# Linear attention feeding an MLP: steps 9 to 12 of the attention in three visits to TensorE instead of four

## The chip, the cores and the metric

The kernel runs on one NeuronCore of a Trainium2 chip. The metric is the time of one execution on the device in microseconds (us), as the median of several runs; lower is better.

## What is computed

The inputs are q, k and v of shape (4, 8, 768, 64) (batch, heads, positions, head size), a decay `lam` per head, and two weight matrices of 512 x 2048 and 2048 x 512. Block by block of 64 positions a causal linear attention with decay is taken, which carries a state of 64 x 64 per batch and head:

```python
for b in range(nb):
    sl = slice(b * block, (b + 1) * block)
    qb, kb, vb = (q[:, :, sl], k[:, :, sl], v[:, :, sl])
    intra = np.einsum('bhic,bhjc->bhij', qb, kb) * Dmask[None]
    intra = np.einsum('bhij,bhjd->bhid', intra, vb)
    inter = np.einsum('bhid,bhde->bhie', qb * lam_pow[None], kv_state)
    out[:, :, sl] = intra + inter
    kb_dec = kb * rev_pow[None]
    kv_state = lam_block * kv_state + np.einsum('bhsd,bhse->bhde', kb_dec, vb)
```

Its output, as 3072 rows of 512, goes through `gelu_tanh(x @ w_in) @ w_out`, and that is the result.

## The kernel before

**The attention** is cut into 24 steps. Step s holds 256 positions of one batch for four of the eight heads; an even step and the odd one after it are the two halves of the heads. Three pairs of steps make a batch (`NSB` = 3), so steps 6 to 11 are batch 1, and steps 10 and 11 are its last positions. Inside a step, two chunks c = 0 and 1 of 128 positions follow each other through the state.

A step is made of: loads of q, k and v (`load_step`, all issued by SP's DMA queue); a scaling of q into fp16 on DVE and a copy of k on ACT (`cast_q` L282, `cast_k` L295); a scaling of v on POOL (`scale_v` L266); a transpose of q and k by DMA into a `qkT` tile (L303); the scores on TensorE (`scores` L350, two PSUM banks); the causal mask (`causal` L360, two DVE instructions, one for each bank); the outputs, that is masked scores times v (L399, or L436 in a burst), and the old state times q (L408, or L461); k times v for the new state (L385, or L450); the state update (`update`: `t` on DVE L506 and `u`, its masked fp16 copy, on POOL L513); and a copy of the outputs to an `xT` tile on ACT (`x_out` L487). For the last positions of a batch the second chunk's k times v is not computed.

TensorE visits the attention in one of two ways. `R(n, s)` (L902) is a single visit: scores of step n, k times v of step n, outputs of an earlier step s, with two banks for the scores and two (`OK`) for the rest. `burst(ns, ss)` (L415) takes several steps together: the scores of all steps in `ns`, then the outputs of all steps in `ss`, then k times v of all in `ns`, then the old states; its tiles are two banks of scores per step, two `O` and two `K`. Within a visit most matmuls use 64 x 64 tiles of the array, four of them at a time; the old states (L408, L461) and the whole MLP use 128 x 128.

**The MLP** works on groups of steps: group 0 is steps 0 to 3, group 1 steps 4 and 5, group 2 steps 6 and 7, group 3 steps 8 to 11, and so on. A group is queued as soon as its outputs are there (`queue_group` L544), as a list of pieces (`filler`). Groups 1 and 2 have eight pieces of the first matrix (`mm1` L557: 8 matmuls of 128x256 into one `Hps` bank, then a gelu on ACT, L565) and seven pieces of the second (`product` L616, a Winograd scheme: 8 matmuls of 128x256 each, L640). The products come in the order 1, 2, 5, 6, 3, 7, 4. Products 1, 6, 7 and 4 add up in one and the same bank, `MX`: after 1, 6 and 7, and at the end after 4, ACT copies the sum out (L657), and each of these products waits for the copy before it. Products 2 and 5, 3 use the banks `MW` and `MY`. `sum_g` (L610) makes sums of gelu results on DVE for the products, `sum_win` (L151) sums of the first matrix on DVE for the last two groups.

**The order** is written by hand: the kernel body is a sequence of calls, and `fill(n)` (L898) puts the next n pieces of the queue at its place. Every engine works through its own instructions in that order. All PSUM tiles come from one pool of eight banks, `ps_M`; a new tile waits for the readers of the tile that had its bank.

The change lies in the loop of L1017 to L1058, which handles steps 8 to 12:

```python
FILL = {8: (2, 0, 0, 0), 9: (1, 2, 1, 2), 10: (0, 1, 1, 3), 11: (0, 1, 1, 3), 12: (0, 2, 1, 3)}
for n, (a, b, c, d) in FILL.items():
```

For n = 9 this puts product 6 of group 1 ahead of the preparation of step 11, then products 3 and 7, then the visit `R(9, 8)`, then product 4 and two `Hps` pieces of group 2. One more `Hps` piece leads to `R(10, 9)`, five more to `R(11, 10)`, products 1, 2, 5, 6, 3 and 7 of group 2 to `R(12, 11)`, and product 4 follows that one.

Of the kernel before, what the change touches and what calls it, by code (L numbers as in the profile page):

```python
# [15 lines left out]
def kernel(  # L16
# [10 lines left out]
    nc = tc.nc  # L27
# [108 lines left out]
    def w_in_block(t, cs, fs):  # L136

        if t in I_SUMS:
            return wi_sum[(t - 1) // 2][:, (t - 1) % 2, cs, fs]
        F, C = t  # L140
        return w_in16[:, 2 * C + cs.start : 2 * C + cs.stop,
                      F * DFF // 2 + fs.start : F * DFF // 2 + fs.stop]

    def sum_win(m, j, eng):

        if not wi_sum:
            wi_sum.extend(wst.tile([P, 2, 2, DFF // 2], FP16, tag=f"w{2 + i}", name=f"ws{i}")
                          for i in range(2))
        a, op, b = I_SUMS[m]
        cs, fs = slice(0, 2), slice(512 * j, 512 * j + 512)  # L150
        pin(eng.tensor_tensor(w_in_block(m, cs, fs), w_in_block(a, cs, fs),  # L151
                              w_in_block(b, cs, fs), op))
# [116 lines left out]
    def prep_qk(s):  # L269
        cast_qk(s)  # L270
        transpose_dma(s)
# [5 lines left out]
    def cast_q(s):  # L277
        q32 = ld32[s][0]
        tqk = a16p.tile([P, 2, 2, HH, D], FP16, tag="qk16", name=f"qk16_{s}")
        tq, tk = tqk[:, 0], tqk[:, 1]  # L280
        q_eng = nc.gpsimd if s == 3 else nc.vector
        pin(q_eng.tensor_tensor(wide(tq), q32[:], decay(dq, s), ALU.mult))  # L282
        if s == 0:
            inverse(halves[0])
            odd(halves[1])
            inverse(halves[1])
        a16[s] = (tq, tk)
        whole_qk[s] = tqk
# [50 lines left out]
    def half64(i):  # L339
        return slice(64 * i, 64 * i + 64)  # L340
# [3 lines left out]
    def scores(n):  # L344
        o = qkT[n]
        Sps = [ps_M.tile([P, 2, 2, P], FP32, tag="M", name=f"S{hl}") for hl in range(2)]
        for hp in range(2):
            for jk in range(2):
                for hl, c in TILES:
                    pin(nc.tensor.matmul(  # L350
                        Sps[hl][half64(c), hp, jk, :], o[half64(hl), 1, jk, hp, half64(c)],
                        o[half64(hl), 0, :, hp, half64(c)], start=True, stop=True,
                        skip_group_check=True))
        Ss[n] = Sps

    def causal(n):

        t = ptp.tile([P, 2, 2, 2, P], FP16, tag="PT", name=f"PT_{n}")
        for hl, Sps in enumerate(Ss.pop(n)):
            pin(nc.vector.tensor_tensor(  # L360
                t[:, hl].rearrange("p b c d -> p b (c d)"), Sps[:].rearrange("p b c d -> p b (c d)"),
                mask[:].unsqueeze(1).to_broadcast([P, 2, 2 * P]), ALU.mult))
        PTs[n] = t
# [51 lines left out]
    def burst(ns, ss, *mix, ahead=None):  # L415


        for i, n in enumerate(ns):
            scores(n)
            if ahead and i == 0:  # L420
                ahead()
        O = [ps_M.tile([P, 2, 2, P], FP32, tag="M", name=f"O{c}") for c in range(2)]
        seen = set()

        def start(kind, c, hl):
            new = (kind, c, hl) not in seen
            seen.add((kind, c, hl))
            return new

        qTs = [qkT.pop(s) for s in ss]  # L430
        for i, s in enumerate(ss):
            PT, tv = PTs.pop(s), a16.pop(s)[2]
            for hp in range(2):
                for jk in range(2):
                    for c, hl in TILES:
                        pin(nc.tensor.matmul(  # L436
                            O[c][half64(hl), i, hp, :], tv[half64(c), jk, 2 * hp + hl, :],
                            PT[half64(c), hl, hp, jk, :], start=start("O", c, hl), stop=False,
                            skip_group_check=True))
        if ns:  # L440
            K = [ps_M.tile([P, 2, P], FP32, tag="M", name=f"K{c}") for c in range(2)]
        for i, n in enumerate(ns):
            _, tk, tv = a16[n]
            last = (n // 2) % NSB == NSB - 1
            for jk in range(2):
                for hp in range(2):
                    for c, hl in TILES:
                        if c == 1 and last:
                            continue
                        pin(nc.tensor.matmul(  # L450
                            K[c][half64(hl), i, hp * D : hp * D + D],
                            tk[half64(c), jk, 2 * hp + hl, :], tv[half64(c), jk, 2 * hp + hl, :],
                            start=start("K", c, hl), stop=(jk == 1), skip_group_check=True))
            Kps[n] = [t[:, i] for t in K]
        for i, s in enumerate(ss):
            for c in range(2):
                if c == 0 and (s // 2) % NSB == 0:
                    continue
                u = us.pop((s, 0) if c else (s - 2, 1))
                for hp in range(2):  # L460
                    pin(nc.tensor.matmul(O[c][:, i, hp, :], u[:, hp].rearrange("p l d -> p (l d)"),  # L461
                                         qTs[i][:, 0, :, hp, half64(c)], start=False, stop=True,
                                         skip_group_check=True))
        for n in ns:
            causal(n)
        for i, s in enumerate(ss):
            x_out(s, [t[:, i].rearrange("p h t -> p (h t)") for t in O])
        sbg = ss[-1] // 2
        g, i = group_of[sbg]
        if ss[-1] % 2 == 1 and i == len(groups[g]) - 1:  # L470
            queue_group(g, *mix)
        for n in ns:
            update(n, 0)

    def x_out(s, OK, second=None):
        sbg, half = divmod(s, 2)
        g, i = group_of[sbg]
        if g not in xT:
            xT[g] = xtp.tile([P, 2, len(groups[g]), 2, SB], FP16, tag="xT", name=f"xT_{g}")
        dst = xT[g][:, half, i]  # L480
        for c in range(2):
            d = dst[:, :, c * P : (c + 1) * P].rearrange("p hp (t j) -> p hp j t", j=2)
            o = OK[c][:, 0:256].rearrange("p (hp j t) -> p hp j t", hp=2, j=2)
            if c == 1 and second is not None:
                pin(second.tensor_copy(out=d, in_=o))
            else:
                pin(nc.scalar.activation(out=d, in_=o, func=AF.Copy))  # L487
# [410 lines left out]
    def fill(n):  # L898
        for _ in range(min(n, len(filler))):
            filler.pop(0)()  # L900

    def R(n, s, ahead=None, keep=False):  # L902

        if n is not None:
            scores(n)
        if ahead:
            ahead()
        products(n, s)
        if n is not None:
            causal(n)  # L910
        if s is not None and s % 2 == 1:
            g, i = group_of[s // 2]
            if i == len(groups[g]) - 1 and g > 0:
                queue_group(g)
        if n is not None and not keep:
            update(n, 0)

    def U(n):
        update(n, 1)
# [98 lines left out]
    for n, (a, b, c, d) in FILL.items():  # L1018
        stage_t(n)
        fill(a + (n == 10))  # L1020
        if n == 8:
            cast_q(n + 2)
            fill(1)
            cast_k(n + 2)
            transpose_dma(n + 2)
        else:
            prep_qk(n + 2)
        if n < 11:
            load_step(n + 4, "qkv" if n < 10 else "qk")
        if n == 9:  # L1030
            store_pair(1)
        if n == 11:
            scale_v(13)
            load_step(14, "v")
            load_step(16, "qk")
        elif n == 9:
            scale_v(11)
        elif n == 10:
            scale_v(12)
            load_step(15, "qk")  # L1040
        elif n == 12:
            scale_v(14)
        fill(b + (n == 8) - (n == 10))
        R(n, n - 1, keep=n == 8)
        fill(c)
        if n == 8:
            update(n, 0)
            scale_v(n + 2)
            fill(2)
        U(n)  # L1050
        if n == 12:
            prep_qk(15)
            load_step(15, "v")
            load_step(16, "v")
            scale_v(15)
        fill(d)
        if n > 8:
            sum_win((n - 7) // 2, (n - 1) % 2, nc.vector)  # L1058

    cast_qk(16)  # L1060
    load_step(17, "qk")
# [91 lines left out]
```

## Time and profile before

| | |
|---|---|
| median of 5 runs | 198.88 us (198.76 to 199.51) |
| the profiled execution | 199.11 us |
| its span | 197.3 us, 5913 instructions |
| TensorE busy | 191.5 us, 97% of the span, granted clock 1.00 |
| VectorE (DVE) busy | 153.4 us, 78% |
| ScalarE (ACT) busy | 121.9 us, 62% |
| GpSimd (POOL) busy | 73.4 us, 37% |
| single visits R(9, 8), R(10, 9), R(11, 10), R(12, 11) begin at | 63.99, 68.51, 73.90, 80.16 us |
| stage from 59 to 69 us, busy of 10 us | PE 10.0, DVE 9.46, ACT 5.40, POOL 6.87 |

Times in the profile are of one execution, from the span's start. PE is TensorE, PEld its weight loads, SPq the DMA-issuing queue of SyncE. A timeline row gives start, duration, engine, line, operation, output and inputs, and the number of instructions merged into it; a bracket behind it is the idle time of the engine and what ended it. Matmuls overlap, so the time that a block of them takes is read from the starts of neighbouring rows.

### The profile page before, as it was taken

What the parts mean: (1) busy time and instruction counts of PE and PEld (TensorE: products, weight loads), DVE (VectorE), ACT (ScalarE), POOL (GpSimd) and SP (SyncE); (2) the same over time, 40 slices, a digit from 0 to 9 for tenths busy, and PEclk for the clock granted to TensorE, in tenths of its full rate; (3) what the DMA queues carried; (4) which work ended last, traced back from release to release, by engine and by line L of the source; (5) the groups of instructions that cost most, each with busy time, mean ns of one, the idle gap of its engine ahead of it and who ended that gap; (6) DMA issues with size and microseconds to landing.
All of it is one profiled execution on the core that took longest, in us unless ns stands there. A gap on an engine that the chain in (4) does not pass through costs nothing.

```text
span 197.3 us, 5913 instructions
## 1 busy us (share of the span) xinstructions
PE 191.5 (97%) x2429; PEld 139.9 (71%) x2431; DVE 153.4 (78%) x297; ACT 121.9 (62%) x249; POOL 73.4 (37%) x85
## 2 busy tenths in 40 slices
PE   8979999999999999999999999999999999999993
PEld 2546544456888888654688764578888888888882
DVE  4798632789999889849999947998778996588620
ACT  3664877457774685676845378844768845779221
POOL 6594213557554931069754507165002030002000
PEclk9999999999999999999999999999999999999999
DMA  5999999999999999999996998400220300030205
GB/s 170 293 325 385 385 386 385 286 285 293 253 222 243 261 342 224 214 242 278 234 293 139 270 310 203 93 6 0 53 81 28 107 7 0 0 110 0 106 19 197
DMA packets 62810, 38.13 MB, mean 193 GB/s; under 512 B 18624, under 2 KB 55744, under 8 KB 62784
## 3 DMA queue, kind: packets, MB, share of 16 engines
q1 hardware_dynamic: 62240, 37.50, 74.0%
q8 instruction: 19, 0.31, 0.7%
q10 hardware_dynamic: 544, 0.26, 0.5%
q14 instruction: 7, 0.06, 0.1%
HBM read 27.26 MB, written 6.29 MB: 170 GB/s over the span
## 4 chain that ended last, share of the span: by engine, by line
PE 78%; DMA 12%; SPq 6%; DVE 1%; issue 1%; ACT 0%
PE Hps L561 21%; PE MX L640 18%; PE MY L640 9%; PE HX L739 7%; DMA wi<-in_moe_w_in_dram 7%; DMA k<-in_k_dram 5%; PE MW L640 4%; SPq L70 4%; PE HY L739 4%; PE S L350 3%; PE O2ps L576 3%; PE HW L739 2%; SPq L94 2%; PE OK L408 1%; PE O L461 1%; PE O L436 1%
## 5 line engine op out<-in xcount | busy, mean ns | idle before, releaser
L561 PE MATMUL Hps<-xT,w_in 128*128 128x512 f16 (+1 forms) x288 | 50.5, 332 | 0.0
L513 POOL TENSOR_TENSOR u<-t,lumask 128x256 f16<-128x256 f32 x40 | 30.9, 787 | 41.8 <-DVE t L506 24.1
L561 PEld LDWEIGHTS <-w_in 128*128 128x128 f16 x288 | 27.9, 98 | 19.1 <-DVE w_in L110 0.2
L565 ACT ACTIVATE gT<-Hps 128x512 f16<-128x512 f32 x56 | 33.5, 598 | 11.6 <-PE Hps L561 11.1
L360 DVE TENSOR_TENSOR PT<-S,mask 128x512 f16<-128x512 f32 x48 | 30.3, 681 | 6.7 <-PE S L350 6.7
L266 POOL TENSOR_TENSOR v<-v,dv 128x512 f16<-128x512 f32 x24 | 28.2, 1179 | 15.8 <-DMA v<-in_v_dram 15.5
L640 PEld LDWEIGHTS <-gs 128*128 128x128 f16 x320 | 31.2, 98 | 3.6
L640 PEld LDWEIGHTS <-gT 128*128 128x128 f16 x240 | 23.3, 98 | 3.2 <-ACT gT L565 0.2
L640 PE MATMUL MX<-w_sum,gs 128*128 128x256 f16 x160 | 21.4, 273 | 0.0
L282 DVE TENSOR_TENSOR qk<-q,dq 128x512 f16<-128x512 f32 x23 | 19.9, 867 | 1.3 <-DMA q<-in_q_dram 1.3
L692 POOL TENSOR_TENSOR o<-u,q 128x512 f32<-128x512 f32 (+1 forms) x5 | 5.8, 1154 | 35.1 <-ACT u L657 35.1
L295 ACT ACTIVATE qk<-k 128x512 f16<-128x512 f32 x23 | 14.4, 625 | 7.2 <-DMA k<-in_k_dram 7.0
L610 DVE TENSOR_TENSOR gs<-gT 128x1024 f16<-128x1024 f16 (+1 forms) x24 | 16.2, 681 | 1.5 <-ACT gT L565 1.5
L576 PE MATMUL O2ps<-w_out,gT 128*128 128x512 f16 x64 | 14.6, 379 | 0.0
L487 ACT ACTIVATE xT<-OK 128x256 f16<-128x256 f32 x26 | 9.9, 452 | 6.7 <-PE OK L408 6.2
L739 PEld LDWEIGHTS <-ws 128*128 128x128 f16 x128 | 12.5, 97 | 1.8
L657 ACT ACTIVATE u<-MX 128x256 f32<-128x256 f32 x18 | 6.9, 383 | 10.2 <-PE MX L640 10.2
L487 ACT ACTIVATE xT<-O 128x256 f16<-128x256 f32 x22 | 8.0, 461 | 5.4 <-PE O L461 4.5
L350 PEld LDWEIGHTS <-qkT 64*64 64x64 f16 x384 | 6.0, 106 | 6.9 <-issue 3.2
L576 PEld LDWEIGHTS <-gT 128*128 128x128 f16 x64 | 6.1, 98 | 6.6
L640 PE MATMUL MY<-w_out,gs 128*128 128x256 f16 x80 | 10.7, 273 | 0.0
L640 PE MATMUL MX<-w_sum,gT 128*128 128x256 f16 x80 | 10.4, 273 | 0.0
(96 smaller groups left out, 317.7 us busy)
## 6 DMA issues: line engine op xcount, KB each, us to landing
q<-in_q_dram SPq DMA_DIRECT2D x24, 256.0 KB, 5.1
k<-in_k_dram SPq DMA_DIRECT2D x24, 256.0 KB, 5.2
v<-in_v_dram SPq DMA_DIRECT2D x23, 256.0 KB, 5.2
out_dram<-o SPq DMA_DIRECT2D x23, 256.0 KB, 4.0
wo<-in_moe_w_out_dram SPq DMA_DIRECT2D x4, 1024.0 KB, 9.4
wi<-in_moe_w_in_dram SPq DMA_DIRECT2D x4, 512.0 KB, 7.1
wi<-in_moe_w_in_dram SPq DMA_DIRECT2D x2, 1024.0 KB, 12.9
v<-in_v_dram ACTq DMA_DIRECT2D x1, 256.0 KB, 4.1
```

The costliest lines, as they stand in the source:

```text
L266: pin(nc.gpsimd.tensor_tensor(wide(tv[:]), ld32[s][2][:], decay(dv, s), ALU.mult))
L282: pin(q_eng.tensor_tensor(wide(tq), q32[:], decay(dq, s), ALU.mult))
L295: pin(nc.scalar.activation(out=wide(tk), in_=k32[:], func=AF.Copy))
L360: pin(nc.vector.tensor_tensor(t[:, hl].rearrange("p b c d -> p b (c d)"), Sps[:].rearrange("p b c d -> p b (c d)"), mask[:].unsqueeze(1).t ...
L487: pin(nc.scalar.activation(out=d, in_=o, func=AF.Copy))
L513: pin(nc.gpsimd.tensor_tensor(u[:], state[half][:].unsqueeze(2).to_broadcast([P, 2, 2, D]), lumask[:, 2 * half : 2 * half + 2, :].unsqueez ...
L561: pin(nc.tensor.matmul(by_block(Hps[:, i, :]), w_in16[:, c, f * P : (f + 1) * P], x(c), start=(c == 0), stop=(c == NC - 1)))
L565: pin(nc.scalar.activation(out=dst, in_=Hps[:], func=AF.Gelu_apprx_tanh))
L576: pin(nc.tensor.matmul(O2[tau][0][:], gT[:, f % HF, f // HF, tau * P : (tau + 1) * P], w_out16[:, f, :], start=(n == 0), stop=(n == NF - 1)))
L610: pin(nc.vector.tensor_tensor(g_rows(m, i), g_rows(a, i), g_rows(b, i), op))
L640: pin(nc.tensor.matmul(dst, lhsT, rhs, start=(opens and i == 0), stop=(closes and i == HF - 1), skip_group_check=True))
L739: pin(nc.tensor.matmul(dst[:, i, :], w_in_block(a, slice(c, c + 1), slice(f * P, f * P + P))[:, 0], x_block(b, slice(c, c + 1))[:, 0], sta ...
```

## The change

Visit 9 is dropped. At n = 9 only the pieces, the preparation of step 11 and the sums stay. At n = 10 a burst takes the scores of 9 and 10 and the outputs of 8, and both second-chunk updates come after the next piece. At n = 11 a burst takes the scores of 11 and the outputs of 9 and 10. The visit of n = 12 stays. One `sum_win` moves from n = 10 to n = 9.

```diff
         fill(b + (n == 8) - (n == 10))
-        R(n, n - 1, keep=n == 8)
+        if n == 10:
+            burst((9, 10), (8,))
+        elif n == 11:
+            burst((11,), (9, 10))
+        elif n != 9:
+            R(n, n - 1, keep=n == 8)
         fill(c)
         if n == 8:
             update(n, 0)
             scale_v(n + 2)
             fill(2)
-        U(n)
+        if n == 10:
+            U(9)
+        if n != 9:
+            U(n)
...
         fill(d)
-        if n > 8:
-            sum_win((n - 7) // 2, (n - 1) % 2, nc.vector)
+        if n == 9:
+            sum_win(1, 0, nc.vector)
+            sum_win(1, 1, nc.vector)
+        elif n > 10:
+            sum_win(2, n - 11, nc.vector)
```

## The prediction, made before the result was known

> **What bounds the kernel now.** I read the page first (busy time, chain), then the waits of PE, then PE's timeline in the stage of the change, then ACT, DVE and POOL there. Page:
>
> ```profile
> PE 191.5 (97%) x2429; PEld 139.9 (71%) x2431; DVE 153.4 (78%) x297; ACT 121.9 (62%) x249; POOL 73.4 (37%) x85
> ...
> PE 78%; DMA 12%; SPq 6%; DVE 1%; issue 1%; ACT 0%
> ```
>
> PE is busy 97% of the span and is most of the chain. All the waits of PE:
>
> ```profile
> PE S L350 <- DVE qkT L326: 0.9, 1, 0.9
> PE idle L181 <- PEq L1137: 0.8, 1, 0.8
> PE Tps L321 <- POOL qk L282: 0.4, 1, 0.4
> ```
>
> All three lie before 14 us. Behind that there is no gap in which a later delay could vanish, or from which something could be won: what PE gains or loses at 60 to 80 us stays in the span. PE's timeline around the visit of step 9 (start, us, instruction):
>
> ```profile
> 62.15 1.04 PE L640 MATMUL MY<-w_out,gs 128*128 128x256 f16 x8
> 63.02 1.04 PE L640 MATMUL MX<-w_sum,gs 128*128 128x256 f16 x8
> 63.99 0.42 PE L350 MATMUL S<-qkT 64*64 64x128 f16 x16
> 64.24 0.29 PE L385 MATMUL OK<-v,qk 64*64 64x64 f16 x16
> 64.36 0.40 PE L399 MATMUL OK<-PT,v 64*64 64x128 f16 x16
> 64.69 0.40 PE L408 MATMUL OK<-qkT,u 128*128 128x128 f16 x4
> 64.92 1.04 PE L640 MATMUL MX<-w_sum,gT 128*128 128x256 f16 x8
> ```
>
> The starts tell the time, since the ends overlap. Eight product matmuls take 63.02 - 62.15 = 0.87. The visit takes 64.92 - 63.99 = 0.93, and its first score starts 63.99 - 63.02 - 0.87 = 0.10 later than another product would. The MX rows on both sides are products 7 and 4 of group 1, in one bank. Between them ACT copies that bank:
>
> ```profile
> 64.10 0.39 ACT L657 ACTIVATE u<-MX 128x256 f32<-128x256 f32 x1 [0.84 <-PE MX L640]
> ```
>
> The visit covers this copy: it ends at 64.49, and product 4 begins at 64.92.
>
> **What the Trainium skill says.** "TensorEngine Tiling (Array Packing)", Key Properties: changing the tiling mode drains TensorE. The trace agrees: 0.10 on the way from 128*128 into 64*64, and some 0.11 on the way out (below). "PSUM — Partial Sum Buffer", PSUM bank collisions: two engines must not be in one bank and quadrant at once, so software orders them by semaphores. So product 4 must wait for the copy; in the trace of before that wait is never the last, so none of its rows shows a price. "Perfetto Trace Analysis", Per-engine timelines: ACT's row ends with the write acknowledged, the semaphore's way to another engine comes after it, and a matmul's row starts behind its wait. The only row that shows that way is a DVE one, 0.06:
>
> ```profile
> 12.01 0.41 DVE L326 COPY qkT<-Tps 128x512 f16<-128x512 f16 x1
> ```
>
> ```profile
> 12.48 0.42 PE L350 MATMUL S<-qkT 64*64 64x128 f16 x16 [0.91 <-DVE qkT L326]
> ```
>
> 12.01 + 0.41 = 12.42, and the score starts at 12.48. "TensorE: Matmul & The Clock Gate", HAM oscillation: only idle gaps above some 3.4 us slow PE's clock. Here the granted clock is 1.00 through the 0.91 gap too, so I give a gap of under 1 us no further cost.
>
> **The change part by part.** The matmuls are the same; they stand in two visits in place of three (step 12's is untouched).
>
> 1. *What a visit costs beside its matmuls.* The timeline of a burst of before with two steps in and two out:
>
> ```profile
> 116.49 0.64 PE L350 MATMUL S<-qkT 64*64 64x128 f16 x32
> 116.97 0.62 PE L436 MATMUL O<-PT,v 64*64 64x128 f16 x32
> 117.41 0.42 PE L450 MATMUL K<-v,qk 64*64 64x64 f16 x32
> 117.77 0.62 PE L461 MATMUL O<-qkT,u 128*128 128x128 f16 x8
> 118.22 7.07 PE L561 MATMUL Hps<-xT,w_in 128*128 128x512 f16 x32
> ```
>
> Sixteen scores cost 0.48 / 2 = 0.24 (0.25 in a single visit), 16 outputs 0.22, a state matmul (L461) 0.45 / 8 = 0.057. Sixteen K matmuls cost 64.36 - 64.24 = 0.12 where outputs follow; 32 of them here, before L461, take 0.36, which is 2 x 0.12 and 0.11 for the way back to 128*128. The same 0.11 is in the single visit: 0.33 for 16 outputs. Eight K matmuls of a last block use half the tiles and cost as much as 16: visits of steps 10 and 11, with 8, take 0.93 too.
> Burst of 9 and 10 with outputs of 8: S 0.47, O 0.22, K 0.25, way out 0.11, four states 0.23: 1.28. Burst of 11 with outputs of 9 and 10: 0.25 + 0.44 + 0.12 + 0.11 + 0.46 = 1.38. With two ways in: 2.66 + 0.20 = 2.86. Before: 3 x 0.93 + 0.30 = 3.09. Saved: 0.23.
>
> 2. *The bank wait inside a burst.* A burst takes eight tiles of a pool of eight banks, so its K1 needs the bank of the last Hps piece ahead of it, whose gelu runs 0.11 to 0.71 behind the burst's start. K starts at 0.47 + 0.22 = 0.69; with 0.06 for the signal it is 0.08 late. The burst of 13 and 14 has the same pattern: its gelu and its K rows are
>
> ```profile
> 87.35 0.60 ACT L565 ACTIVATE gT<-Hps 128x512 f16<-128x512 f32 x1 [0.27 <-PE Hps L561]
> ```
>
> ```profile
> 87.94 0.50 PE L450 MATMUL K<-v,qk 64*64 64x64 f16 x32
> 88.37 0.28 PE L461 MATMUL O<-qkT,u 128*128 128x128 f16 x2
> ```
>
> 0.43 for K in place of 0.36. I take 0.07 for the burst of 9 and 10 (bounds 0 and 0.15); the burst of 11 has long finished pieces ahead of its banks. Saved is now 0.23 - 0.07 = 0.16 (bounds 0.05 and 0.30).
>
> 3. *The cover that goes.* The visit of step 9 is where the single visit stood between products 7 and 4. With it gone, product 4 follows product 7 at once: it would start at 63.02 + 0.87 = 63.89. But the copy still cannot begin before product 7's last matmul is through, 64.10, and ends at 64.49; with 0.06, product 4 starts at 64.55. PE stands still for 0.66. Bounds: 0.60 (a signal that takes nothing) and 0.75 (0.15 for it). Queued behind it on PE are three Hps pieces and the burst; ACT's gelus, DVE's causal rows and so everything of the later stages wait for those. The same pair of group 2 keeps its cover, the untouched visit of 12 (79.20 product 7, 80.16 visit, 81.10 product 4).
>
> 4. *What is moved on the other queues, taken at nothing.* DVE: causal 9 (2 x 0.64) and its four state updates go behind two ws sums (L151, one moved forward from step 10) and the q cast of step 12. From 64.5: two sums of up to 0.96, then the cast, 1.10 in the trace and started at 67.34 there; free by 68.5 at the latest. The burst's first scores are ready at about 68.13 + 0.46 = 68.6, so the cover is 0.1 or more; without it each 0.1 costs 0.1, for the first Hps piece behind the burst (1.35 after its start) needs the bank of the first causal row (0.46 + 0.68 + 0.06 = 1.20). After that DVE has 2.5 of causal rows and 1.2 of updates before the next burst, 5.7 later, and its gs sums for group 2 finish earlier against PE than before. POOL: u of 9 and 10 (3 x 0.8) now stand behind v of step 12 (to 69.34), are done by about 74 and are first read at about 74.9; the step 13 v behind them is wanted at 87. ACT: the outputs of 8, 9 and 10 come 4 to 5 us later and are read by group 3 only, at 82; four of them, 1.4, end at 76.9, and the copy of product 1 behind them is needed at 78.0. SP's order is the same; qkT, qk and v buffers come free up to 5 us later, and their next writers (qkT of 13 at 76.0, v of 13 at 71.7) come after that.
>
> Sum: + 0.66 - 0.16 = + 0.50. The profiled execution took 199.11 (span 197.3 and 1.8 around it), which lies 0.23 above the median of 198.88, inside the runs' 198.76 to 199.51. So 199.61 for such an execution, and 199.4 against the median, 0.25% slower.
>
> **Rivals.** *A, not slower.* A visit's fixed price is larger than the rows say, because the matmul ends are modelled and a drain is spread over neighbours. Place: both mode changes; price in my reading 0.10 + 0.11 and 0.02. It decides from 0.66 + 0.07 = 0.73 per visit on. Against it: the burst's sums above reproduce 1.73 to 0.02. At 0.8 per visit the time is 198.8. *B, half covered.* The saving is at its upper bound (no K1 wait, cheaper second visit: 0.30) and the stall at its lower one (0.60): + 0.30, 199.2. For it: 0.06 was seen for DVE only. *C, a new wait at the burst.* DVE, busy 9.5 of 10 us at 59 to 69, comes late with causal 9, or POOL's u rows do, and the burst with all eight banks stops PE by another 0.3 to 0.5: 199.8. For it: q of step 12 is loaded only just before its cast. That the edit leaves the order as it was is excluded: in the program as built, product 4 stands right behind product 7 and its first matmul waits for ACT's copy.
>
> **How the numbers follow.** Main case (stall 0.66, one visit won) 0.68; A 0.06; B 0.13; C 0.13. A measurement of this kernel can tell about 0.2%, 0.4 us, from no change, so the forecast lies close to that line: of the main case about a quarter falls below 199.28. Slower: 0.51 + 0.13 = 0.64; within: 0.17 + 0.13 + 0.03 = 0.33; faster: half of A, 0.03. Range: 199.05 leaves out A and the lowest part of B, 199.75 half of C.
>
> **What would show it.** Right: in PE's waits a new row, MX L640 behind ACT u L657, near 0.6; product 4 starting 0.06 behind ACT's copy; bursts of about 1.35 and 1.38; the visit of step 12 0.5 later than 80.16, and every later stage by the same. Wrong: product 4 at 63.9; single rows of PE waiting for DVE at the first Hps behind the burst (C); a shift that changes after 81 us.

## The result, and the profile after

The changed kernel takes 199.51 us (median of 28 runs, 199.3 to 200.95), the kernel before 198.94 us in runs beside it (47 runs, 198.76 to 199.76). The ratio is 1.004 with a 95% interval of 1.0031 to 1.005: it is slower. The ratios leave out slow executions, of which the kernels tried below had one, of 201.94 us with the new order of products. Three further sets of runs of the same changed kernel, told below, gave medians of 199.41, 199.47 and 199.35 us. The profiled execution took 199.31 us, with a span of 197.5 us (before: 199.11 and 197.3).

The page of the changed kernel, first its row of busy time, then the engines' shares of the chain that ended last:

```profile
PE 191.1 (97%) x2429; PEld 140.2 (71%) x2431; DVE 155.2 (79%) x297; ACT 121.8 (62%) x249; POOL 74.8 (38%) x85
...
PE 89%; SPq 4%; DMA 4%; ACT 1%; issue 0%
```

TensorE has the same 2429 matmuls and is busy 0.4 us less in a span that is 0.2 us longer: it stands still somewhere. The larger share of PE in the chain (89% in place of 78%) has nothing to do with the change. In the execution of before the chain leaves PE at about 40 us, for a load of k; in this one PE is on it from 18 us on.

The waits of PE in the changed kernel (engine, what waited, for whom: us in total, times, longest):

```profile
PE S L350 <- DVE qkT L326: 1.1, 2, 0.8
PE idle L181 <- PEq L1148: 0.8, 1, 0.8
PE MX L640 <- ACT u L657: 0.5, 1, 0.5
PE Tps L321 <- POOL qk L282: 0.5, 1, 0.5
PE Hps L830 <- ACT w_in L108: 0.3, 1, 0.3
```

The third row is the new one that matters: a product matmul waits once for ACT's copy of bank `MX`. All others lie before 20 us, where loads come at slightly different times in each execution. PE's timeline shows the place:

```profile
62.79 1.04 PE L640 MATMUL MX<-w_sum,gs 128*128 128x256 f16 x8
64.30 1.03 PE L640 MATMUL MX<-w_sum,gT 128*128 128x256 f16 x8 [0.47 <-ACT u L657]
65.17 2.78 PE L561 MATMUL Hps<-xT,w_in 128*128 128x256 f16 x24
67.88 0.64 PE L350 MATMUL S<-qkT 64*64 64x128 f16 x32
68.35 0.39 PE L436 MATMUL O<-PT,v 64*64 64x128 f16 x16
68.58 0.50 PE L450 MATMUL K<-v,qk 64*64 64x64 f16 x24
69.01 0.40 PE L461 MATMUL O<-qkT,u 128*128 128x128 f16 x4
69.24 4.53 PE L561 MATMUL Hps<-xT,w_in 128*128 128x256 f16 x40
73.70 0.42 PE L350 MATMUL S<-qkT 64*64 64x128 f16 x16
...
75.08 1.04 PE L640 MATMUL MX<-w_out,gT 128*128 128x256 f16 x8
...
80.41 0.42 PE L350 MATMUL S<-qkT 64*64 64x128 f16 x16
```

And ACT's timeline has the copy between the first two rows:

```profile
63.86 0.38 ACT L657 ACTIVATE u<-MX 128x256 f32<-128x256 f32 x1 [0.84 <-PE MX L640]
```

Product 7 starts at 62.79 and would hand over after 0.87, at 63.66. The copy runs from 63.86 to 64.24 and product 4 starts at 64.30. PE loses 64.30 - 63.66 = 0.64. The bracket says 0.47, because it counts from the modelled end of product 7's last matmul; what the stall costs is read from the starts.

The visit of step 12 starts at 80.41, 0.25 later than before. But this execution was ahead when it came to the change: product 7 starts at 62.79, before at 63.02, and the first `Hps` piece of the stage stood at 49.06 against 49.29. The 0.23 has nothing to do with the change: at 24.23 us both executions start the same row together, and the one of before falls behind at 39 us, where its chain runs through a load of k. From product 7 on the change costs 0.25 + 0.23 = 0.48. Nothing is won back or added later: the burst of 13 and 14 starts 0.25 later (87.49 against 87.24), and the last block of products 0.24 later (190.74 against 190.50).

### The profile page after: what moved, and what is told of

It is laid out like the page before. It is cut to its first block, busy times and chain, and to the rows that moved or that the text cites. A ratio compares the mean times of both kernels' runs of the same rounds, so it can differ in the third digit from the quotient of the medians.

```text
span 197.5 us, 5913 instructions
## 1 busy us (share of the span) xinstructions
PE 191.1 (97%) x2429; PEld 140.2 (71%) x2431; DVE 155.2 (79%) x297; ACT 121.8 (62%) x249; POOL 74.8 (38%) x85
## 4 chain that ended last, share of the span: by engine, by line
PE 89%; SPq 4%; DMA 4%; ACT 1%; issue 0%
PE Hps L561 25%; PE MX L640 18%; PE MY L640 9%; PE HX L739 7%; PE O2ps L576 7%; PE MW L640 4%; DMA wi<-in_moe_w_in_dram 4%; SPq L70 4%; PE HY L739 4%; PE S L350 3%; PE Hps L830 3%; PE O L461 2%; PE HW L739 2%; PE O L436 2%; PE OK L408 1%; PE Tps L321 1%
## 5 line engine op out<-in xcount | busy, mean ns | idle before, releaser
L513 POOL TENSOR_TENSOR u<-t,lumask 128x256 f16<-128x256 f32 x40 | 31.4, 801 | 40.0 <-DVE t L506 26.4
L692 POOL TENSOR_TENSOR o<-u,q 128x512 f32<-128x512 f32 (+1 forms) x5 | 6.5, 1308 | 34.8 <-ACT u L657 34.8
L610 DVE TENSOR_TENSOR gs<-gT 128x1024 f16<-128x1024 f16 (+1 forms) x24 | 17.2, 722 | 1.0 <-ACT gT L565 1.0
L487 ACT ACTIVATE xT<-O 128x256 f16<-128x256 f32 x28 | 10.1, 460 | 6.2 <-PE O L461 5.3
L487 ACT ACTIVATE xT<-OK 128x256 f16<-128x256 f32 x20 | 7.6, 451 | 5.8 <-PE OK L408 5.3
L610 DVE TENSOR_TENSOR gs<-gT,gs 128x1024 f16<-128x1024 f16 (+1 forms) x12 | 10.4, 870 | 0.3
```

The source lines that it names most:

```text
L513: pin(nc.gpsimd.tensor_tensor(u[:], state[half][:].unsqueeze(2).to_broadcast([P, 2, 2, D]), lumask[:, 2 * half : 2 * half + 2, :].unsqueez ...
L610: pin(nc.vector.tensor_tensor(g_rows(m, i), g_rows(a, i), g_rows(b, i), op))
```

## The experiments

The theory is the prediction's: losing the cover of the `MX` copy costs 0.6 to 0.7 us, and one visit less, with a short bank wait, gives 0.16 back. Its rivals were A (a visit costs more, the two cancel), B (half of the stall is hidden) and C (a new wait at the bursts). Every median below stands against the kernel before in the same set of runs.

### The changed kernel again

No edit.

> The changed kernel once more, on the chip of the other three, for a second trace. My theory (the uncovered copy between products 7 and 4 of group 1 costs 0.63 us, one visit saved wins about 0.15): 0.4 to 0.6 us above the kernel before for most executions, product 4 starting 0.05 to 0.07 us behind ACT's copy. Its runs spread further upwards (199.3 to 200.95) than those of before: if a second wait appears only in some executions, a trace of one above 199.9 shows a wait of PE that the first trace does not have; if the spread is outside the kernel, the others of this call have it too.

Measured: 199.41 us (7 runs), before 198.99; ratio 1.0029 (1.0018 to 1.004). In its trace product 4 follows the copy by the same stall, and the bursts take 1.36 and 1.38 us again. So the difference repeats from one set of runs to another.

### The lost cover alone

The kernel before, with product 4 ahead of the visit of step 9. All four single visits stay.

```diff
-    FILL = {8: (2, 0, 0, 0), 9: (1, 2, 1, 2), 10: (0, 1, 1, 3), 11: (0, 1, 1, 3), 12: (0, 2, 1, 3)}
+    FILL = {8: (2, 0, 0, 0), 9: (1, 3, 0, 2), 10: (0, 1, 1, 3), 11: (0, 1, 1, 3), 12: (0, 2, 1, 3)}
```

> The kernel before with its four single visits, only that product 4 of group 1 is put ahead of visit 9 and not behind it: the cover is lost and nothing is won. My theory: PE waits 0.6 us for ACT u L657, the time is 0.55 to 0.7 above before, that is more than the changed kernel's. Rival (the bursts cost the time, for instance by taking all eight banks): no more than 0.1 above before.

Measured: 199.49 us (5 runs), before 198.99; ratio 1.0031 (1.0019 to 1.0043). The median is 0.50 above before, a little less than the 0.55 to 0.7 that was expected, and five runs do not tell it from the changed kernel's 199.41 in the same set. PE's timeline in this kernel:

```profile
62.94 1.04 PE L640 MATMUL MX<-w_sum,gs 128*128 128x256 f16 x8
64.45 1.03 PE L640 MATMUL MX<-w_sum,gT 128*128 128x256 f16 x8 [0.47 <-ACT u L657]
65.41 0.42 PE L350 MATMUL S<-qkT 64*64 64x128 f16 x16
```

The stall is 64.45 - 62.94 - 0.87 = 0.64, to the hundredth that of the changed kernel, with no burst in sight. One product moved past one visit is enough to make the kernel about as slow as the change does; the table below has the difference that the medians do not resolve. Rival B put it at 0.60 and needs a saving of 0.30 beside it, which the next runs measure.

### The change without the lost cover, and the edit for it alone

If the copy is the cost, another product between 7 and 4 should cover it. Product 3 writes `MY`. I changed the order for group 1 only, in the changed kernel and, as a control, in the kernel before; the last two sums of gelu results on DVE change places so that product 7's comes first.

```diff
-        order = [(m, p) for m in (1, 2, 5, 6, 3, 7, 4) for p in range(HN // P)]
+        turn = (1, 2, 6, 5, 7, 3, 4) if g == 1 else (1, 2, 5, 6, 3, 7, 4)
+        order = [(m, p) for m in turn for p in range(HN // P)]
...
-            behind(9, 4, 8, (4,))
-            behind(10, 4, 8, (3,))
+            behind(9, 4, 8, (3,) if g == 1 else (4,))
+            behind(10, 4, 8, (4,) if g == 1 else (3,))
```

In the changed kernel:

> The changed kernel, with the products of group 1 in the order 1, 2, 6, 5, 7, 3, 4 in place of 1, 2, 5, 6, 3, 7, 4, so that each copy out of MX runs beside a product in another bank, with no visit needed between 7 and 4 (the sums for products 7 and 3 change places too). My theory: no wait of PE for ACT u, the loss of 0.63 goes and what stays is the saved visit: 0.1 to 0.2 below before. Rival (the loss is in the bursts): as slow as the changed kernel.

In the kernel before:

> The kernel before with the same order of the products of group 1 as in the run with the changed kernel and reordered products. There the copy is covered by the visit anyway. Both theories: within 0.1 of before; if it is faster or slower by more, the new order does something else too and the difference to the changed kernel with it has to be read against this one.

In the changed kernel, a second time:

> The changed kernel with the products of group 1 in the order 1, 2, 6, 5, 7, 3, 4 a second time: most runs at 198.7 to 198.85, some at 199.2 to 199.6 by either theory; its trace, if it is a slower one, tells the two apart as for the changed kernel.

Measured: the changed kernel with the new order takes 198.82 us (14 runs, before 198.99, ratio 1.0001, 0.9992 to 1.0011) and the second time 198.78 us (14 runs, before 198.96, ratio 0.999, 0.9982 to 0.9998). The kernel before with the new order takes 198.97 us (13 runs, before 198.99, ratio 0.9999, 0.999 to 1.0007): by itself the order does nothing, because there the visit already covered the copy between 7 and 4. PE's timeline of the changed kernel with the new order, second time, then its ACT:

```profile
61.96 1.04 PE L640 MATMUL MX<-w_sum,gs 128*128 128x256 f16 x8
62.83 1.04 PE L640 MATMUL MY<-w_out,gs 128*128 128x256 f16 x8
63.71 1.04 PE L640 MATMUL MX<-w_sum,gT 128*128 128x256 f16 x8
```

```profile
63.03 0.38 ACT L657 ACTIVATE u<-MX 128x256 f32<-128x256 f32 x1
```

The copy is over at 63.41 and product 4 starts at 63.71, with no wait: product 3's 0.87 covers it, with 0.30 left between the end of the copy and product 4. The wait for ACT is gone from PE's waits.

The traces give the parts of the sum more sharply than the medians. From the start of the product ahead of product 4 (or, in the two kernels with the visit there, of the last product ahead of that visit) to the first scores of the burst of 13 and 14, every kernel has the same matmuls to do. These rows end the stretch in before, changed, before with the cover lost, and changed with the new order (again):

```profile
87.24 0.64 PE L350 MATMUL S<-qkT 64*64 64x128 f16 x32
87.49 0.64 PE L350 MATMUL S<-qkT 64*64 64x128 f16 x32
87.79 0.64 PE L350 MATMUL S<-qkT 64*64 64x128 f16 x32
86.90 0.64 PE L350 MATMUL S<-qkT 64*64 64x128 f16 x32
```

The whole table:

| kernel | from | to | us | against before |
|---|---|---|---|---|
| before | 63.02 | 87.24 | 24.22 | |
| before, new order | 62.75 | 86.97 | 24.22 | 0.00 |
| before, cover lost | 62.94 | 87.79 | 24.85 | + 0.63 |
| changed, new order | 62.79 | 86.85 | 24.06 | - 0.16 |
| changed, new order, again | 62.83 | 86.90 | 24.07 | - 0.15 |
| changed | 62.79 | 87.49 | 24.70 | + 0.48 |
| changed, again | 62.89 | 87.59 | 24.70 | + 0.48 |

The two parts add up: 0.63 - 0.16 = 0.47. In the seven traces of the next section, whose edits leave TensorE's work in this stretch as it is, it takes 24.69 or 24.70 where product 4 follows 7 (five traces) and 24.06 or 24.07 with the new order (two). A change with a gain of 0.16 was turned into a loss by one product standing in the wrong place. With the new order the changed kernel takes 198.78 us and without it 199.47 us in one set of runs, 0.35% less. Against the kernel before its medians are 0.17 and 0.18 us lower, which agrees with the 0.16 of the traces; but of the two intervals of its ratio one takes in no change, and the other (0.9982 to 0.9998) only just leaves it out. Rival A needs a visit price that equals the stall, 0.73 instead of 0.23: it falls, since with the stall gone only 0.15 to 0.16 is won. The same number leaves rival B, which needs 0.30, without ground. Rival C falls because the two parts leave no room in this stretch for another wait.

### The scatter of the changed kernel

Of 60 runs of the changed kernel in four sets, 20 lie above 199.75 us, up to 200.95; of the 155 runs of the kernel before in all five sets, 19 lie as far (0.3 us) above the median of their set. I looked for what makes these executions long. First, the changed kernel itself once more, and a version with one DVE sum for group 3 moved to a later piece:

```diff
-            behind(9, 0, 4, (1, 2) if g == 3 else (1, 2, 4, 3))
+            behind(9, 0, 4, (1,) if g == 3 else (1, 2, 4, 3))
             if g == 3:
-                behind(12, 0, 4, (4, 3))
+                behind(12, 0, 4, (2, 4, 3))
```

The changed kernel:

> The changed kernel a third time, beside the run with one sum later, for the spread of its runs and for a trace of a slower one. Theory S (a second, occasional wait: in the burst of 15 and 16 DVE comes to its causal rows too late, because a gs sum or the q cast of step 17 ahead of them was held up by POOL's v of 15 and 16): 199.3 to 199.5 for most runs, some at 199.7 to 200.9, and a trace of such a run has the first Hps piece behind the burst of 15 and 16 waiting for DVE. Theory D (the spread comes from the loads before 40 us): the trace of a slower run is late before 40 us already.

The changed kernel with the sum moved:

> The changed kernel with one of DVE's two gs sums of group 3 (about 0.95 us) moved from ahead of the causal rows of 15 and 16 to behind them. Theory S: the slower runs go, all within 199.3 to 199.55. Theory D: the spread is that of the changed kernel, a third of the runs above 199.7.

The new order with the sum moved:

> Both: the products of group 1 reordered and one gs sum behind the causal rows of 15 and 16. If theory S holds and the saved visit is worth 0.15 us: all runs at 198.7 to 198.9, 0.1 to 0.2 below the kernel before, and so faster than both kernels. By theory D a third of the runs stays at 199.2 and above, and the mean is that of before.

Measured: 199.47 us (18 runs, 5 above 199.75; ratio 1.0029, 1.0016 to 1.0042), 199.48 us (10 runs, 3 above; ratio 1.0028, 1.0013 to 1.0043) and 198.78 us (14 runs; ratio 0.9989, 0.998 to 0.9998), with 198.96 for before. Moving the sum took no long run away, so the theory of the sum falls. But the profiled execution of the first was itself a long one, 200.43 us, and it has a wait that none of the other profiled executions shows. Among its waits of PE:

```profile
PE S L350 <- DMA qkT<-qk: 0.8, 1, 0.8
```

Its PE timeline, at the burst of 15 and 16:

```profile
94.15 0.42 PE L350 MATMUL S<-qkT 64*64 64x128 f16 x16
95.35 0.42 PE L350 MATMUL S<-qkT 64*64 64x128 f16 x16 [0.78 <-DMA qkT<-qk]
```

The scores of step 16 come 95.35 - 94.15 = 1.20 behind those of step 15 where they take 0.24: 0.96 lost. They wait for the DMA transpose of step 16. The queue of SP ahead of that, in this execution:

```profile
86.31 2.72 SPq L70 DMA_DIRECT2D q<-in_q_dram  x1
89.08 0.51 SPq L70 DMA_DIRECT2D k<-in_k_dram  x1
89.74 1.41 SPq L303 DMA_TRANSPOSE qkT<-qk  x1
91.25 0.52 SPq L70 DMA_DIRECT2D v<-in_v_dram  x1
```

I took the load of q of step 17 for the cause: it held SP for 2.72 us (0.51 in the profiled execution after the change, 1.83 in that of before), so that the transpose was issued only at 89.74. The execution with the sum moved, which does not wait at this place, speaks against that as the whole reason:

```profile
86.66 0.51 SPq L70 DMA_DIRECT2D q<-in_q_dram  x1
87.21 0.51 SPq L70 DMA_DIRECT2D k<-in_k_dram  x1
87.87 3.37 SPq L303 DMA_TRANSPOSE qkT<-qk  x1
91.34 0.52 SPq L70 DMA_DIRECT2D v<-in_v_dram  x1
```

Here the load of q is short and the transpose's own issue long, and SP is through with it at 91.24, later than 91.15 in the long execution. Yet the transpose has landed 6.1 us after the start of its issue, at about 94.0, and in the long execution 5.6 us after it, at about 95.3. From the end of the issue to the landing that is 2.7 us against 4.2. So what was unusual in the long execution came behind the issue, and why that transfer took longer stays open. An earlier issue should cover it all the same. The next edit changes the places of the two:

```diff
     cast_qk(16)
+    transpose_dma(16)
     load_step(17, "qk")
-    transpose_dma(16)
```

The changed kernel with this swap, the new order and the moved sum with it, the swap once more, and the changed kernel beside that:

> The changed kernel with one edit in SP's queue: the transpose of step 16 is issued ahead of the load of q and k of step 17, not behind it. In one execution of the changed kernel, 200.43 us long, PE stood 0.96 us at the second scores of the burst of 15 and 16 for that transpose, whose issue came late because the load of q of step 17 took 2.72 us ahead of it (0.51 to 1.83 in other executions). Theory T, that this is what makes the long executions: all runs within 199.2 to 199.6, none over 199.7 (in the unedited kernel a third are), median 199.4. Theory V, that the long executions have several sources: the share over 199.7 stays at a quarter or more. A cost of the edit itself: q of step 17 comes about 1.4 to 3.5 us later, its cast on DVE (93.9 us) would then wait and hold causal 15 up; if so the median rises to 199.8 or more and a new PE wait shows at 95 us.

> The same edit in the kernel with the products of group 1 reordered and the one sum moved. Theory T: median 198.7 to 198.8 as without it, and no run over 199.1. Theory V: median the same and the spread the same (198.6 to 199.4). A cost of the edit: 199.1 or more, with a PE wait at 95 us behind the cast of q of step 17.

> The changed kernel with the transpose of step 16 ahead of the load of q and k of step 17, a second time. In the first time none of 9 runs was over 199.7 us, where 17 of 53 runs of the changed kernel are. Theory T (the long executions come from that transpose): again none over 199.7, median 199.4 to 199.5. Theory V (several sources): a quarter or more of the runs over 199.7.

> The changed kernel itself, in the same set of runs as a control: both theories expect a median of 199.4 to 199.5 and about a third of the runs over 199.7, up to 201. If there are none, this chip and hour make no long executions, and the run beside it tells nothing.

Measured: with the swap 199.49 us (9 runs, 199.33 to 199.69; ratio 1.0025, 1.0015 to 1.0035) and 199.57 us (10 runs, 199.38 to 199.72; ratio 1.0029, 1.002 to 1.0038). The changed kernel beside the second of these: 199.35 us (7 runs, 199.28 to 199.96, two above 199.75; ratio 1.0025, 1.0014 to 1.0036). The new order, moved sum and swap: 198.79 us (13 runs, 198.66 to 199.44; ratio 0.9992, 0.9984 to 1.0). In the swapped kernel SP issues the transpose first:

```profile
86.40 3.52 SPq L303 DMA_TRANSPOSE qkT<-qk  x1
89.98 0.57 SPq L70 DMA_DIRECT2D q<-in_q_dram  x1
```

None of the 19 runs of the changed kernel with the swap is above 199.75 (one, at 199.72, is above the expected limit of 199.7), against 20 of 60 without it. This does not show that the late transpose makes the long executions. The sets with the swap were quiet ones: of the runs of the kernel before in them 1 of 37 lies 0.3 us above its median, against 18 of 118 in the other three, and only seven runs of the changed kernel stood beside the swap. And with the swap and the new order one run took 199.44 us, where the theory expected none over 199.1. That one was profiled, and has no wait at 95 us: at 24 us it is already 0.66 late (24.77, where the second profiled execution with the new order stands at 24.11). The profiled execution with the sum moved, 199.79 us, is of the same kind: 24.86 against 24.23 in the first one of the changed kernel, and product 7 at 63.28 in place of 62.79. So there are several sources, of which the late transpose was seen once.

The swap itself wins nothing in the median, 199.49 and 199.57 against 199.35 to 199.51. The cost that I had feared, q of step 17 arriving too late for its cast, does not show: in none of the three profiled executions with the swap does PE or that cast wait for a load at 92 to 96 us. In one of them the `Hps` piece behind the burst starts 0.25 late, after DVE's mask rows, which came late behind a DVE sum of 1.49 us. Why the changed kernel meets long executions more often than the kernel before stays open. One more trait of long executions: of the runs whose mean granted clock is known, all ten at 0.991 (five of the kernel before, five of changed ones) lie 0.5 us or more above the median of their kernel in the set. But most of the changed kernel's long executions, 18 of 20, have 0.997 or more.

## Why the prediction was right

The forecast was 199.4 us; the four sets gave 199.35 to 199.51.

1. *The visit's price* (0.23 saved). The two bursts were put at 1.35, with the bank wait, and 1.38. They take 69.24 - 67.88 = 1.36 and 75.08 - 73.70 = 1.38. The way into the first is 67.88 - 65.17 - 24 x 0.109 = 0.09, where 0.10 was used. Steps 1 and 2 together were put at 0.16, and the kernel with the new order shows 0.15 to 0.16.

2. *The bank wait inside the burst* (0.07). The K rows of the first burst take 69.01 - 68.58 = 0.43 where 24 of them with the way out would take 0.36. The 0.07 fits. No run took this wait away by itself, but the trace agrees with the account. The gelu of the last piece ahead of the burst ends at 68.59:

```profile
67.99 0.60 ACT L565 ACTIVATE gT<-Hps 128x512 f16<-128x512 f32 x1 [0.28 <-PE Hps L561]
```

Of the K matmuls, taken one by one, the first starts at 68.58 and the second not before 68.64, 0.05 behind that gelu; in the burst of 11 the first two start 0.01 apart.

3. *The cover that goes* (0.66; 0.64 measured). The copy of `MX` starts 0.03 behind the modelled end of product 7 (63.83) and ends after 0.38, and product 4 starts 0.06 after that. The prediction had 0.39 for the copy, and took the 0.06 for the signal from a DVE row, on the reading of the Trainium skill, "Perfetto Trace Analysis", Per-engine timelines, that the semaphore's way comes behind ACT's row; this trace now shows the same 0.06 for ACT.

4. *What moves on the other queues* (nothing). DVE's timeline after, at the burst of 9 and 10:

```profile
68.34 2.48 DVE L360 TENSOR_TENSOR PT<-S,mask 128x512 f16<-128x512 f32 x4 [0.83 <-PE S L350]
```

DVE stood idle for 0.83 and waited for PE's scores, so the cover that the prediction put at 0.1 or more was larger, and the first `Hps` piece behind the burst starts at 69.24 without a wait. POOL:

```profile
71.29 2.25 POOL L513 TENSOR_TENSOR u<-t,lumask 128x256 f16<-128x256 f32 x3 [2.06 <-DVE t L506]
```

The `u` rows end at 73.54; they were put at about 74, and the first reader, the old states of the second burst, comes at 74.62. No new wait on SP's queue shows in this execution. What the step did not see is the scatter: in one of four profiled executions of the changed kernel a transpose landed so late that TensorE waited 0.96 for it at 95 us. The prediction took SP's queue at one execution's durations.

One reading of the prediction was not exact: it said that behind 14 us there is no gap of PE in the kernel before. At 39 us that execution does lose time, in waits that the list of waits does not have: its row of eight transposes takes 0.71 from start to start (39.00 to 39.71) where the changed kernel's takes 0.45 (38.90 to 39.35). This belongs to the 0.23 between the two executions and leaves the argument as it is, for it lies ahead of the change's stage.

The sum of the steps was + 0.50, and the trace has + 0.48; the medians of the four sets lie 0.40 to 0.57 above before. The point that decided was which product follows which in the same bank, and its place was found in the timeline of the kernel before: a visit that looked like a cost of 0.93 hid 0.64 of waiting.

## What to carry to other kernels

Before a piece of work is taken out from between two others, look at what runs on the other engines under it: two accumulations in one PSUM bank with a copy between them need something else on TensorE for as long as the end of the first, the copy and the signal take, here 0.64 us. If the piece has to go, put another one there; here a product into a different bank did it, and the saving of the removed visit, about 0.16 us, came through. A combination that saves a fixed price per visit is worth at most that price (put at 0.23 us here, of which 0.15 to 0.16 came through), so the first thing to price is what the removed visit covered.

## What the runs showed of the hardware that was not expected

- SP's issue of one and the same 256 KB load of q took 0.51, 1.59, 1.83 and 2.72 us in four executions, and that of one and the same DMA transpose 1.39 to 3.67 us. The two can balance: with the load at 0.51 and the transpose at 3.52 the next load was issued at 91.02, with 2.72 and 1.41 at 91.25.
- The end of a DMA's issue does not tell when it lands: of two executions in which SP was through with the same transpose at 91.24 and 91.15, it landed at about 94.0 in the first and about 95.3 in the second, which cost TensorE 0.96 us.
- With the granted clock at 1.00 the stall of 0.64 us left no trace behind it: the product after it took 0.87 us again (64.30 to 65.17).
- Parts of the PE timeline repeat to 0.01 us in different executions and kernels (the stall 0.64, the bursts 1.36 and 1.38), while executions are up to 0.75 us apart at 24 us already (24.11 to 24.86), behind the first loads.
